# First 512 tokens through three transposing loads instead of matrix turns, in a fused linear-attention and dense-layer kernel

## The chip, the cores and the metric

The kernel runs on one core of a Trainium2 chip. The metric is the device time of one execution in microseconds, as the median of several runs. A core has five engines with instruction queues of their own: TensorE (PE, matmuls; PEld is its loading of weights), VectorE (DVE), ScalarE (ACT), GpSimd (POOL) and SyncE (SP). DMAs are issued here from SP's and ACT's queues; an engine that issues one is held for the time of the issue, and the data lands later.

## The reference

`x` is 2048 x 512 (tokens by features), in bf16, as all inputs are.

```python
g = sigmoid((x * gate_w).sum(-1, keepdims=True))
# A: linear attention, 32 heads of 16
q, k, v = heads(x @ wqkv)
phi(t) = concat(softmax(t @ w_phi), softmax(-(t @ w_phi)))   # per head, 16 + 16 features
kv = einsum("hsf,hsd->hfd", phi(k), v);  z = phi(k).sum(over s)
a = (phi(q) @ kv) / (phi(q) @ z + 1e-6)  @ wo
# B: a dense layer
b = relu(x @ w1) @ w2          # w1: 512 x 1376, w2: 1376 x 512
out = g * a + (1 - g) * b
```

## The kernel before

The 2048 tokens are 16 tiles of 128, or four chunks of 512. Every matmul over features needs `x` with the features on the partitions: that is the tile `XT` (128 partitions, 4 row pieces `j` of 128 features, 2048 tokens).

Each step is a named task on one engine, with its dependencies. The order of the tasks on each engine is written out in `ORDER`, one string an engine; a planner found it beforehand, and the numbers `dur`, `lat` and `boost` in the tasks are what it used. They are not read when the kernel is built: `schedule` only looks up the names, `number` gives each task a semaphore and a count (an engine's own semaphore, or one of its own for each DMA), and `emit` puts the waits ahead of the task. So an engine runs its tasks strictly in the order of its string, and a task that waits holds up all that stands behind it on the same engine; DMA issues stand in the strings of SP and ACT as well.

The tasks that matter here:

- `warm0` (line 258): matmuls of ones on PE, six of 512 columns, before any data is there.
- `x00` to `x03` (`load_x`, line 272): plain loads of the first four tiles of tokens into `XN`, a corner of `FT`, with the tokens on the partitions.
- `xt{m}{n}` (`pe_xt`, line 350): two matmuls each with the identity `IDN`, which turn two of the four 128 x 128 blocks of tile `m` into PSUM. `xe{m}{n}` (lines 362 on ACT, 365 on DVE) copy them into `XT`.
- `w1a0` to `w1a3`: the first 512 columns of `w1`, one load for each row piece `j`; `w1b` and `w1c` the other columns.
- `hh00` to `hh3` (`pe_h_first`, line 403): the four first units of `x @ w1` (512 of the 1376 columns), for tokens 0 to 255, row piece by row piece. `h0_0` to `h0_3` (`pe_h_rest`, line 409): the same units for tokens 256 to 511. `h{c}_{k}` (`pe_h`, line 397): the other units, chunk `c`, columns `k`. `rl*` (line 454, ACT) apply the relu and write `HT`.
- `f1_*`, `f0_*` (`pe_fold`, line 374): fold `w_phi`, made block-diagonal in `WBD`, into the key and query columns of `wqkv`, which `wkT` and `wqT` bring in transposed (`load_t`, line 277, an `dma_start_transpose`). `fe*` evict them into `WP`.
- `pr_*` (line 496): the folded projections of pairs of tiles, keys (`k0` to `k8`) and then queries (`q0` to `q8`); `ev` (523, ACT), `mx` and `mn` (527, 529, DVE), `t1` and `t2` (536, POOL), `ex` (541, ACT), `sm` and `rc` (DVE) and `nm` (550 and 573, POOL) make the two softmaxes of them. `v*` (476) and `kv*` (557) build `kv` and `z`.
- `tq*` (576) and `to*` (614): transposing DMAs from SBUF to SBUF, of 128 x 1024 and of 128 x 512 elements. `nd*` (600), `b*` (622), `a*` (628): attention output, second dense layer and `wo`, tile by tile. `oe*` and `st*` evict and store.

Chunks 1 to 3 of `x` come in by `load_t` as 512 tokens each (`x1`, `x2`, `x3`), straight into `XT`.

The turns of the first tokens and the copies behind them:

```python
XB, FB = ((0, 1), (6, 7), (0, 1), (6, 7)), (0, 1, 6, 7)

def pe_xt(q, m, n):
    for j in range(2 * n, 2 * n + 2):
        last = q.matmul(PS[:, XB[m][j // 2], (j % 2) * P:(j % 2 + 1) * P], XN[:, m, j * P:(j + 1) * P],
                        IDN[:, :], start=True, stop=True)
    return last
```

Of the kernel before, what the change touches and what calls it, by code (L numbers as in the profile page):

```python
# [6 lines left out]
ALU = mybir.AluOpType  # L7
# [42 lines left out]
    ),  # L50
# [98 lines left out]
def bass_gated_mix__linear_kernel_hedgehog__dense_activation_relu__prompt_kernel(  # L149
# [34 lines left out]
    WARM = (6 * (512,),)  # L184
# [3 lines left out]
    with ExitStack() as es:  # L188
# [32 lines left out]
        COLI = sb("COLI", [P, P], I32)  # L221
        IDN = sb("IDN", [P, P], BF16)
# [24 lines left out]
        add("iota_i", "pool", lambda q: q.iota(COLI[:, :], [[1, P]], channel_multiplier=0), dur=0.25, boost=800.0)  # L247
# [4 lines left out]
        XN = FT[:, NF - 2, :].rearrange("p (m d) -> p m d", d=D)  # L252
# [40 lines left out]
        load_x(0, "sp", 2.95)
        load_x(1, "act", 3.1)
        load_w(0, "sp", 3.2)
        load_w(1, "act", 3.4)
        load_w(2, "sp", 3.8)
        load_w(3, "act", 3.95)
        load_x(2, "sp", 4.0)
        load_x(3, "sp", 3.9)  # L300
        load("w1b", "sp", W1[:, :, 512:1024], w1r[:, :, 512:1024], dur=0.5, lat=5.0)
        load("wphi", "sp", WPS[:, :, :], A_w_phi.rearrange("(g hl) r c -> (hl r) g c", g=ND), dur=0.5, lat=4.9)
        load_t("wkT", WT[:, ND:2 * ND, :], A_wqkv[:, D:2 * D], (), 4.1, 2.7)
        load("w1c", "sp", W1[:, :, 1024:DFF], w1r[:, :, 1024:DFF], dur=0.5, lat=4.0)
        load("wv", "sp", WV[:, :, :], wvr, dur=0.5, lat=4.9)
        g.follow("iota_r", "iota_i")
        g.follow("iota_i", "iota_c")
        load_t("x1", XT[:, :, chunk(1)], x2[chunk(1), :], ("w1c",), 2.6, 2.3)
# [11 lines left out]
        add("ident", "dve", lambda q: q.tensor_tensor(IDN[:, :], ROWH[:, :], COLI[:, :], ALU.is_equal),  # L320
            ("iota_r", "iota_i"), dur=0.3, boost=2000.0)
# [12 lines left out]

        def pe_turn(q, b, blocks):
            for n, src in enumerate(blocks):
                last = q.matmul(PS[:, b, n * P:(n + 1) * P], src, IDN[:, :], start=True, stop=True)
            return last

# [6 lines left out]
        XB, FB = ((0, 1), (6, 7), (0, 1), (6, 7)), (0, 1, 6, 7)  # L346

        def pe_xt(q, m, n):
            for j in range(2 * n, 2 * n + 2):
                last = q.matmul(PS[:, XB[m][j // 2], (j % 2) * P:(j % 2 + 1) * P], XN[:, m, j * P:(j + 1) * P],  # L350
                                IDN[:, :], start=True, stop=True)
            return last

        for m in range(4):
            for n in range(2):
                add(f"xt{m}{n}", "pe", lambda q, m=m, n=n: pe_xt(q, m, n),
                    (f"x0{m}", "ident", f"xe{m - 2}{n}" if m > 1 else None), dur=0.2, boost=9000.0 - 10 * m)
            for n, eng in enumerate(("act", "dve")):
                xo = XT[:, 2 * n:2 * n + 2, m * P:(m + 1) * P]
                xi = PS[:, XB[m][n], 0:2 * P].rearrange("p (j t) -> p j t", j=2)  # L360
                if eng == "act":
                    add(f"xe{m}{n}", eng, lambda q, o=xo, i=xi: q.activation(o, i, ACT.Copy), (f"xt{m}{n}",), dur=0.35,
                        boost=9000.0 - 10 * m)
                else:
                    add(f"xe{m}{n}", eng, lambda q, o=xo, i=xi: q.tensor_copy(o, i), (f"xt{m}{n}",), dur=0.37,  # L365
                        boost=9000.0 - 10 * m)
        x0 = [f"xe{m}{n}" for m in range(4) for n in range(2)]
        xof = [x0, ["x1"], ["x2"], ["x3"]]


        HB = (3, 4, 5)
        def pe_fold(q, s, j, b):
            for i in range(ND):
                last = q.matmul(PS[:, b, i * P:(i + 1) * P], WT[:, s * ND + i, j * P:(j + 1) * P], WBD[:, i, :],  # L374
                                start=True, stop=True)
            return last

        for j in range(ND):
            b = FB[j]
# [361 lines left out]
```

## Time and profile before

| | |
|---|---|
| median of 3 runs | 151.77 us (151.59 to 152.13) |
| profiled execution: time, span | 151.63 us, 150.1 us |
| granted TensorE clock | 1.0 |
| PE busy | 145.3 us, 97% of the span |
| POOL, DVE, ACT busy | 109.4, 113.3, 92.2 us |
| PE's share of the chain that ended last | 94% |
| DMA | 15.59 MB, mean 104 GB/s |

The span is that of the instructions on the core; the execution's own time is longer by what lies around it. Lines such as L350 are lines of the kernel. "DMA ... to landing" counts from the start of an issue to the last of its 16 arrivals.

### The profile page before, as it was taken

What the parts mean: (1) busy time and instruction counts of PE and PEld (TensorE: products, weight loads), DVE (VectorE), ACT (ScalarE), POOL (GpSimd) and SP (SyncE); (2) the same over time, 40 slices, a digit from 0 to 9 for tenths busy, and PEclk for the clock granted to TensorE, in tenths of its full rate; (3) what the DMA queues carried; (4) which work ended last, traced back from release to release, by engine and by line L of the source; (5) the groups of instructions that cost most, each with busy time, mean ns of one, the idle gap of its engine ahead of it and who ended that gap; (6) DMA issues with size and microseconds to landing.
All of it is one profiled execution on the core that took longest, in us unless ns stands there. A gap on an engine that the chain in (4) does not pass through costs nothing.

```text
span 150.1 us, 2498 instructions
## 1 busy us (share of the span) xinstructions
PE 145.3 (97%) x936; PEld 74.3 (49%) x953; DVE 113.3 (76%) x168; ACT 92.2 (61%) x127; POOL 109.4 (73%) x71
## 2 busy tenths in 40 slices
PE   7999999999999999999999999999999999999992
PEld 2774444445554465445444545455444454454461
DVE  2423666999899949969999999999999969436301
ACT  3356769799969766599983937446564551310151
POOL 3000499999999999999999999998999791330000
PEclk9999999999999999999999999999999999999999
DMA  4999991000005603400000230975659884766251
GB/s 144 302 261 239 163 231 23 0 0 0 7 1 112 238 0 54 120 0 0 4 0 0 60 82 15 116 159 135 174 106 155 195 213 105 146 171 144 65 163 52
DMA packets 46307, 15.59 MB, mean 104 GB/s; under 512 B 39796, under 2 KB 46292, under 8 KB 46296
## 3 DMA queue, kind: packets, MB, share of 16 engines
q1 hardware_dynamic: 43560, 12.99, 42.1%
q10 hardware_dynamic: 2736, 2.45, 5.0%
q8 instruction: 7, 0.11, 0.3%
q14 instruction: 4, 0.03, 0.1%
HBM read 4.42 MB, written 2.11 MB: 43 GB/s over the span
## 4 chain that ended last, share of the span: by engine, by line
PE 94%; DMA 2%; issue 1%; DVE 1%
PE PS L622 24%; PE PS L397 23%; PE PS L496 18%; PE PS L476 9%; PE PS L628 9%; PE PS L557 3%; PE PS L600 3%; DMA FT<-in_A_x_dram 2%; PE PS L643 2%; PE PS L409 1%; PE PS L374 1%; PE PS L403 1%; PE PS L350 1%; PE PS L654 1%; DVE XT L365 1%
## 5 line engine op out<-in xcount | busy, mean ns | idle before, releaser
L536 POOL TENSOR_TENSOR TS<-PB,MX 128x1024 bf16<-128x1024 bf16 (+1 forms) x18 | 30.8, 1719 | 14.9 <-DVE MX L527 14.9
L397 PE MATMUL PS<-XT,W 128*128 128x512 bf16 (+1 forms) x156 | 38.3, 379 | 0.2
L622 PE MATMUL PS<-W,HT 128*128 128x512 bf16 (+1 forms) x160 | 37.5, 379 | 0.3
L543 DVE TENSOR_REDUCE ZB<-FT 128x128 f32<-128x2048 bf16 (+1 forms) x18 | 36.5, 2030 | 0.7 <-ACT FT L541 0.6
L541 ACT ACTIVATE FT<-TS 128x2048 bf16<-128x2048 bf16 (+1 forms) x18 | 30.9, 1718 | 7.7 <-POOL TS L536 7.5
L536 POOL TENSOR_TENSOR TS<-MN,PB 128x1024 bf16<-128x1024 bf16 (+1 forms) x18 | 30.9, 1723 | 0.8 <-DVE MN L529 0.8
L496 PE MATMUL PS<-WP,XT 128*128 128x512 bf16 x124 | 30.0, 379 | 0.2
L550 POOL TENSOR_TENSOR FT<-FT,SC 128x2048 bf16<-128x2048 bf16 (+1 forms) x9 | 29.5, 3286 | 0.0
L454 ACT ACTIVATE HT<-PS 128x512 bf16<-128x512 f32 (+1 forms) x44 | 24.7, 597 | 6.1 <-PE PS L397 4.9
L622 PEld LDWEIGHTS PS<-W,HT 128*128 128x128 bf16 (+1 forms) x165 | 15.5, 98 | 17.1
L527 DVE TENSOR_REDUCE MX<-PB 128x64 bf16<-128x1024 bf16 (+1 forms) x18 | 19.5, 1084 | 5.8 <-ACT PB L523 5.7
L397 PEld LDWEIGHTS PS<-XT,W 128*128 128x128 bf16 (+1 forms) x160 | 15.6, 101 | 16.5
L673 ACT ACTIVATE OSB<-PS,OMG 128x512 bf16<-128x512 f32 x15 | 10.2, 686 | 22.1 <-PE PS L628 22.1
L529 DVE TENSOR_REDUCE MN<-PB 128x64 bf16<-128x1024 bf16 (+1 forms) x18 | 19.3, 1083 | 2.6 <-ACT PB L523 2.6
L523 ACT ACTIVATE PB<-PS 128x1024 bf16<-128x1024 f32 (+1 forms) x18 | 16.7, 926 | 6.4 <-PE PS L496 3.4
L496 PEld LDWEIGHTS PS<-WP,XT 128*128 128x128 bf16 x128 | 12.1, 98 | 13.9 <-DVE WP L344 0.4
L573 POOL TENSOR_TENSOR FT<-FT,SR 128x1024 bf16<-128x1024 bf16 (+1 forms) x9 | 15.6, 1735 | 0.7
L476 PE MATMUL PS<-WV,XT 128*128 128x512 bf16 x62 | 16.0, 379 | 0.1
L628 PE MATMUL PS<-WO,OT 128*128 128x512 bf16 x58 | 14.2, 378 | 0.1
L609 DVE SCALAR_TENSOR_TENSOR OTM<-PS,EG,RD 128x256 bf16<-128x256 f32 x32 | 13.8, 462 | 0.2
L607 DVE RECIPROCAL RD<-PS 128x16 f32<-128x16 f32 x32 | 6.5, 234 | 9.0 <-PE PS L600 8.8
L485 ACT ACTIVATE VS<-PS 128x512 bf16<-128x512 f32 x16 | 9.6, 602 | 4.8 <-PE PS L476 4.7
(50 smaller groups left out, 97.5 us busy)
## 6 DMA issues: line engine op xcount, KB each, us to landing
out_dram<-OSB ACTq DMA_DIRECT2D x15, 128.0 KB, 2.2
W<-in_B_w_dram SPq DMA_DIRECT2D x1, 1280.0 KB, 6.9
W<-in_B_w_dram SPq DMA_DIRECT2D x1, 512.0 KB, 4.6
WV<-in_A_wqkv_dram SPq DMA_DIRECT2D x1, 512.0 KB, 4.6
WO<-in_A_wo_dram SPq DMA_DIRECT2D x1, 512.0 KB, 5.1
FT<-in_A_x_dram SPq DMA_DIRECT2D x3, 128.0 KB, 3.2
W<-in_B_w_dram SPq DMA_DIRECT2D x1, 352.0 KB, 3.8
W<-in_B_w_dram ACTq DMA_DIRECT2D x2, 128.0 KB, 3.3
```

Of the source, the lines that this page charges most:

```text
L397: last = q.matmul(PS[0:m, b, :], W1[:, j, k * P:k * P + m], XT[:, j, chunk(c)], start=(j == 0), stop=(j == ND - 1))
L454: add(f"rl{a}_{k}", "act", lambda q, a=a, k=k, b=b, rows=rows: q.activation(HT[0:rows, k, chunk(a)], PS[0:rows, b, :], ACT.Relu), (prev,), ...
L476: last = q.matmul(PS[:, 2, :], XT[:, j, m * P:(m + 1) * P], WV[:, j, :], start=(j == 0), stop=(j == ND - 1))
L496: last = q.matmul(PS[:, n, :], XT[:, j, m * P:(m + 1) * P], WP[:, s, j, :], start=(j == 0), stop=(j == ND - 1))
L527: add(f"mx_{J}", "dve", lambda q, sl=sl, w=w, i=pbg: q.tensor_reduce(MX[:, sl, 0:w * H], i, AX.X, ALU.max), (f"ev_{J}", old("t1")), dur=0. ...
L529: add(f"mn_{J}", "dve", lambda q, sl=sl, w=w, i=pbg: q.tensor_reduce(MN[:, sl, 0:w * H], i, AX.X, ALU.min), (f"ev_{J}", old("t2")), dur=0. ...
L536: add(f"{tn}_{J}", "pool", lambda q, o3=o3, a3=a3, b3=b3: q.tensor_tensor(o3, a3, b3, ALU.subtract), (f"{'mx' if sg == 0 else 'mn'}_{J}", ...
L541: add(f"ex_{J}", "act", lambda q, fs=fs, ts=ts, w=w: q.activation(FT[:, fs, 0:w * F], TS[:, ts, 0:w * F], ACT.Exp), (f"t1_{J}", f"t2_{J}", ...
L543: add(f"sm_{J}", "dve", lambda q, fs=fs, sl=sl, w=w: q.tensor_reduce(ZB[:, sl, 0:2 * w * H], FT[:, fs, 0:w * F].rearrange("p (g d) -> p g ...
L550: add(f"nm_{J}", "pool", lambda q, f3=f3, sl=sl, w=w: q.tensor_tensor(f3, f3, SC[:, sl, 0:2 * w * H].unsqueeze(2).to_broadcast([P, 2 * w * ...
L622: last = q.matmul(PS[:, ab, :], HT[0:r, k, m * P:(m + 1) * P], W2[0:r, k, :], start=(k == 0), stop=False)
L628: last = q.matmul(PS[:, ab, :], OT[:, m % NOT, t, :], WO[:, t, :], start=False, stop=(t == ND - 1))
```

## The change

Tiles 0 to 3 of the tokens no longer come in by four plain loads and sixteen matmuls. Three transposing loads write `XT` directly: `x00` (tile 0), `x01` (tile 1) and `x023` (tiles 2 and 3). With them go `XN`, the identity (`iota_i`, `ident`, `IDN`), `pe_xt` and the eight evictions. The transposing loads stand on SP's queue, with `w1a1` and `w1a3` between them; `w1a0` and `w1a2` are issued from ACT, and so are now `wphi`, which waits for `x01`, and `w1c`, which waits for `w1b`. The first units are split into eight tasks `hh{m}{j}`, by tile `m` and row piece `j`, in the order 00 02 01 10 12 11 03 13. There are seven warming matmuls instead of six. All five orders are written anew: on PE, `h0_7` now stands ahead of `pr_k0`, and the first `v` units come earlier. SP waits for four more stores at the end, all of them older than the last.

```diff
-        "x00 w1a0 w1a2 x02 x03 w1b wphi wkT w1c wv x1 x2 wqT x3 gw ...            # sp
+        "x00 w1a1 x01 w1a3 x023 w1b wkT wv x1 x2 wqT x3 gw ...
-        "x01 w1a1 w1a3 xe00 xe10 xe20 xe30 rl0_0 rl0_1 rl0_3 rl0_2 fe1_1 fe1_3 ...   # act
+        "w1a0 w1a2 wphi rl0_0 rl0_1 w1c rl0_2 rl0_4 rl0_5 fe1_1 fe1_3 rl0_3 ev_k0 ...
-        "warm0 xt00 xt01 xt10 xt11 hh00 hh01 hh1 hh2 xt20 xt21 xt30 xt31 hh3 h0_0 h0_1 h0_2 h0_3 h0_4 h0_5 f1_0   # pe
-        "f1_1 f1_2 f1_3 h0_6 pr_k0 h0_7 h0_8 pr_k1 h0_9 h1_0 pr_k2 ...
+        "warm0 hh00 hh02 hh01 hh10 hh12 hh11 hh03 hh13 h0_0 h0_1 h0_2 h0_3 h0_4 h0_5 h0_6 f1_2 f1_1 f1_0 f1_3 "
+        "h0_7 pr_k0 v0 h0_8 pr_k1 h0_9 v1 pr_k2 v2 h1_0 h1_1 pr_k3 ...
...
-    WARM = (6 * (512,),)
+    WARM = (7 * (512,),)
...
-        def load_x(m, eng, lat):
-            load(f"x0{m}", eng, XN[:, m, :], x0r[:, m, :], dur=0.45, lat=lat)
+        def load_x(name, t0, t1, dur, lat):
+            load_t(name, XT[:, :, t0 * P:t1 * P], x2[t0 * P:t1 * P, :], (), dur, lat)
...
+        load_w(0, "act", 2.0)
+        load_w(2, "act", 2.0)
+        load_x("x00", 0, 1, 0.9, 2.1)
+        load_w(1, "sp", 2.05)
+        load_x("x01", 1, 2, 0.9, 1.75)
+        load_w(3, "sp", 1.7)
+        load_x("x023", 2, 4, 1.34, 1.5)
+        load("wphi", "act", WPS[:, :, :], A_w_phi.rearrange("(g hl) r c -> (hl r) g c", g=ND), ("x01",), dur=0.5, lat=2.45)
...
+        load("w1c", "act", W1[:, :, 1024:DFF], w1r[:, :, 1024:DFF], ("w1b",), dur=0.5, lat=3.2)
...
-        x0 = [f"xe{m}{n}" for m in range(4) for n in range(2)]
-        xof = [x0, ["x1"], ["x2"], ["x3"]]
+        xof = [["x00", "x01", "x023"], ["x1"], ["x2"], ["x3"]]
...
-        add("hh00", "pe", lambda q: pe_h_first(q, 0, 0, P), ("xe00", "w1a0"), dur=0.22, boost=8500.0)
-        add("hh01", "pe", lambda q: pe_h_first(q, 0, P, 2 * P), ("xe10", "hh00"), dur=0.22, boost=8500.0)
-        prev = "hh01"
-        for j in range(1, ND):
-            add(f"hh{j}", "pe", lambda q, j=j: pe_h_first(q, j, 0, 2 * P), (f"xe0{j // 2}", f"xe1{j // 2}", f"w1a{j}", prev), dur=0.44,
-                boost=8500.0)
-            prev = f"hh{j}"
+        steps = [(m, j) for js in ((0, 2, 1), (3,)) for m in range(2) for j in js]
+        prev = None
+        for m, j in steps:
+            add(f"hh{m}{j}", "pe", lambda q, m=m, j=j: pe_h_first(q, j, m * P, (m + 1) * P), (f"x0{m}", f"w1a{j}", prev),
+                dur=0.22, boost=8500.0)
+            prev = f"hh{m}{j}"
...
-            for m in range(NT - NOS - 2, NT - 1):
+            for m in range(NT - NOS - 6, NT - 1):
                 q.wait_ge(sems[f"st{m}"], 16)
```

More of the change, by code (lines that the diff above doesn't have):

```diff
@@ L220, in bass_gated_mix__linear_kernel_hedgehog__dense_activation_relu__prompt_kernel @@
         COLH = sb("COLH", [P, P], I32)
-        COLI = sb("COLI", [P, P], I32)
-        IDN = sb("IDN", [P, P], BF16)
         ROWS = sb("ROWS", [P, P], I32)
@@ L246, in bass_gated_mix__linear_kernel_hedgehog__dense_activation_relu__prompt_kernel @@
         add("iota_r", "pool", lambda q: q.iota(ROWH[:, :], [[0, P]], channel_multiplier=1), dur=0.25, boost=900.0)
-        add("iota_i", "pool", lambda q: q.iota(COLI[:, :], [[1, P]], channel_multiplier=0), dur=0.25, boost=800.0)
         add("iota_c", "pool", lambda q: q.iota(COLH[:, :], [[1, 8], [0, DH]], channel_multiplier=0), dur=0.25,
@@ L251, in bass_gated_mix__linear_kernel_hedgehog__dense_activation_relu__prompt_kernel @@
             ap(VS, NT * NG * GZ, GV, [[GZ, NT * NG], [1, 1]]), 1.0), dur=0.7, boost=-1e4)
-        XN = FT[:, NF - 2, :].rearrange("p (m d) -> p m d", d=D)
         one = nc.const_aps.tensor(1.0, (P, 1), BF16).tensor
@@ L284, in bass_gated_mix__linear_kernel_hedgehog__dense_activation_relu__prompt_kernel @@
         w1r = B_w1.rearrange("(j p) n -> p j n", p=P)
-        x0r = x2[chunk(0), :].rearrange("(m p) d -> p m d", p=P)
         wvr = A_wqkv[:, 2 * D:3 * D].rearrange("(j p) n -> p j n", p=P)
-        def load_x(m, eng, lat):
-            load(f"x0{m}", eng, XN[:, m, :], x0r[:, m, :], dur=0.45, lat=lat)
+        def load_x(name, t0, t1, dur, lat):
+            load_t(name, XT[:, :, t0 * P:t1 * P], x2[t0 * P:t1 * P, :], (), dur, lat)
         def load_w(j, eng, lat):
             load(f"w1a{j}", eng, W1[:, j, 0:512], w1r[:, j, 0:512], dur=0.45, lat=lat)
[L293 to L308, printed above, removed]
+        load_w(0, "act", 2.0)
[6 more added lines that the diff above has]
+        load("wphi", "act", WPS[:, :, :], A_w_phi.rearrange("(g hl) r c -> (hl r) g c", g=ND), ("x01",), dur=0.5, lat=2.45)
+        load("w1b", "sp", W1[:, :, 512:1024], w1r[:, :, 512:1024], dur=0.45, lat=2.7)
+        load_t("wkT", WT[:, ND:2 * ND, :], A_wqkv[:, D:2 * D], (), 3.6, 2.0)
+        load("w1c", "act", W1[:, :, 1024:DFF], w1r[:, :, 1024:DFF], ("w1b",), dur=0.5, lat=3.2)
+        load("wv", "sp", WV[:, :, :], wvr, dur=0.5, lat=4.0)
+        g.follow("iota_r", "iota_c")
+        load_t("x1", XT[:, :, chunk(1)], x2[chunk(1), :], ("w1c",), 2.0, 2.8)
         load_t("x2", XT[:, :, chunk(2)], x2[chunk(2), :], (), 2.0, 4.3)
@@ L319, in bass_gated_mix__linear_kernel_hedgehog__dense_activation_relu__prompt_kernel @@
             ("iota_r",), dur=0.25)
-        add("ident", "dve", lambda q: q.tensor_tensor(IDN[:, :], ROWH[:, :], COLI[:, :], ALU.is_equal),
-            ("iota_r", "iota_i"), dur=0.3, boost=2000.0)
         add("blk", "dve", lambda q: q.tensor_tensor(GB[:, :], ROWS[:, :], COLH[:, :], ALU.is_equal),
@@ L332, in bass_gated_mix__linear_kernel_hedgehog__dense_activation_relu__prompt_kernel @@
         wbd = [f"wbd{j}" for j in range(ND)]
[L335 to L338, printed above, removed]
         def evict(name, eng, out_, b, deps, **how):
@@ L344, in evict @@
                 add(name, eng, lambda q: q.tensor_copy(out_, PS[:, b, :]), deps, dur=0.69, **how)
[L346 to L366, printed above, removed]
-        x0 = [f"xe{m}{n}" for m in range(4) for n in range(2)]
-        xof = [x0, ["x1"], ["x2"], ["x3"]]
+        FB = (0, 1, 6, 7)
+        xof = [["x00", "x01", "x023"], ["x1"], ["x2"], ["x3"]]
         HB = (3, 4, 5)
@@ L379, in bass_gated_mix__linear_kernel_hedgehog__dense_activation_relu__prompt_kernel @@
             b = FB[j]
-            war = [f"xe{2 + j // 2}{j % 2}"]
-            add(f"f1_{j}", "pe", lambda q, j=j, b=b: pe_fold(q, 1, j, b), ("wkT", *wbd, *war), dur=0.24,
+            add(f"f1_{j}", "pe", lambda q, j=j, b=b: pe_fold(q, 1, j, b), ("wkT", *wbd), dur=0.24,
                 boost=1800.0)
@@ L414, in bass_gated_mix__linear_kernel_hedgehog__dense_activation_relu__prompt_kernel @@
         GB4 = (*HB, 2)
-        add("hh00", "pe", lambda q: pe_h_first(q, 0, 0, P), ("xe00", "w1a0"), dur=0.22, boost=8500.0)
-        add("hh01", "pe", lambda q: pe_h_first(q, 0, P, 2 * P), ("xe10", "hh00"), dur=0.22, boost=8500.0)
-        prev = "hh01"
-        for j in range(1, ND):
-            add(f"hh{j}", "pe", lambda q, j=j: pe_h_first(q, j, 0, 2 * P), (f"xe0{j // 2}", f"xe1{j // 2}", f"w1a{j}", prev), dur=0.44,
-                boost=8500.0)
-            prev = f"hh{j}"
-        for line in (("warm0", "xt00", "xt01", "xt10", "xt11", "hh00", "hh01", "hh1", "hh2", "xt20", "xt21", "xt30", "xt31",
-                      "hh3"), ("xe00", "xe10", "xe20", "xe30"),
-                     ("ident", "shift", "xe01", "xe11", "xe21", "xe31", "blk", "row4", "mk")):
+        steps = [(m, j) for js in ((0, 2, 1), (3,)) for m in range(2) for j in js]
[4 more added lines that the diff above has]
+            prev = f"hh{m}{j}"
+        g.follow("warm0", "hh00")
+        for line in (("iota_r", "iota_c"), ("shift", "blk", "row4", "mk")):
             for a, b in zip(line, line[1:]):
@@ L538, in bass_gated_mix__linear_kernel_hedgehog__dense_activation_relu__prompt_kernel @@
             war = [(f"kv{m}" if jobs[jn - NF][0] == "k" else f"tq{m}") for m in jobs[jn - NF][1]] if jn >= NF else []
-            if jn == NF - 2:
-                war += [f"xt{m}{n}" for m in range(4) for n in range(2)]
             add(f"ex_{J}", "act", lambda q, fs=fs, ts=ts, w=w: q.activation(
```

67 rows, old and new, of the table ORDER are left out of this document.

## The prediction

> **What bounds the kernel now.** I read the page's first part, then the chain that ended last in its first 13 us, then SP's timeline and the tiles of the transposing loads, and last the table of windows.
>
> The page's first part (engine, busy us, share of the span, instructions):
>
> ```profile
> PE 145.3 (97%) x936; PEld 74.3 (49%) x953; DVE 113.3 (76%) x168; ACT 92.2 (61%) x127; POOL 109.4 (73%) x71
> ```
>
> PE is busy for 145.3 of 150.1 us, so time can only be saved where PE does work that isn't needed, or waits. The windows (us, then each engine's busy time) show that from 9.27 on there is next to none:
>
> ```profile
> 3.57:7.31 3.74, 3.54 (x36) 2.79 (x37) 1.70 (x6) 1.50 (x4) 0.00 (x0) 1.00 1.07 309
> 9.27:20.00 10.73, 10.68 (x61) 5.22 (x62) 4.54 (x5) 7.00 (x12) 3.06 (x2) 1.00 1.08 214
> ```
>
> Over 9.27 to 147.30 PE is busy for 137.12 of 138.03 us by the six windows that cover it: 0.9 idle. After it come 2.80 us in which the last tile is evicted and stored; the change doesn't touch them. So the change is decided by when PE has done its first units. The chain of waits (start, us, what):
>
> ```profile
> 0.74 2.78 DMA FT<-in_A_x_dram
> 3.52 0.05 issue
> 3.57 0.97 PE PS L350 x8
> 4.53 0.30 PE PS L403 x4
> 4.83 0.03 issue
> 4.86 1.27 PE PS L403 x12
> 6.13 0.24 PE PS L350 x4
> 6.37 0.02 issue
> 6.40 0.78 DVE XT L365 x2
> 7.18 0.14 issue
> 7.31 1.91 PE PS L409 x16
> 9.27 1.67 PE PS L397 x7
> ```
>
> A plain load of 128 tokens lands at 3.52; PE turns them (L350), ACT and DVE evict the turned blocks into `XT` (L362, L365), and only then can `hh*` (L403) run. The second half of the tokens goes the same way, and `h0_0` to `h0_3` (L409, tokens 256 to 511) start at 7.31. Call that start T. From T on everything is solid PE work, so the end moves as T does, one for one, unless something new is late behind it.
>
> **The change, part by part.**
>
> *PE's work.* Sixteen turns go. In their place nothing: the 32 pieces of 128 columns of `hh00` to `hh13` do the work of today's 20 (8 of 128, 12 of 256). L374 runs sixteen 128-column matmuls in 0.89 us, 0.056 each, so 32 take 1.79; today's take 8 x 0.056 + 12 x 0.109 = 1.76. The seventh warming matmul costs 0.43 (they start 0.43 apart, the last at 2.86): PE is free at 3.7 instead of 3.3. That is hidden by the wait for x01, w1a3 and x023, which all land later (below); were they early, it would cost 0.1 to 0.4. The eight evictions leave ACT and DVE, which wait at that stage anyway: nothing.
>
> *SP's queue decides T.* It now issues x00, w1a1, x01, w1a3, x023, w1b, wkT in this order; the `x` pieces and wkT are transposing loads. What such an issue costs (ns, min/median/max):
>
> ```profile
> L277 SPq DMA_TRANSPOSE XT<-in_A_x_dram x3: 1792/2319/3222, 11.5 to 19.1; - x3
> L277 SPq DMA_TRANSPOSE WT<-in_A_wqkv_dram x2: 2484/3014/3543, 4.1 to 16.6; - x2
> L576 SPq DMA_TRANSPOSE PHQ<-FT x16: 1231/1312/2256, 84.3 to 134.1; - x16
> L614 SPq DMA_TRANSPOSE OT<-OTM x16: 1188/1210/2272, 92.4 to 141.6; - x16
> L272 SPq DMA_DIRECT2D FT<-in_A_x_dram x3: 414/432/432, 0.7 to 2.6; - x3
> ```
>
> and from issue to landing (page, part 6, median us):
>
> ```profile
> FT<-in_A_x_dram SPq DMA_DIRECT2D x3, 128.0 KB, 3.2
> PHQ<-FT SPq DMA_TRANSPOSE x16, 2.8
> OT<-OTM SPq DMA_TRANSPOSE x16, 2.4
> ```
>
> No row has 128 tokens transposed from DRAM. From below: a quarter of the quickest load of 512 tokens, 1.79 / 4 = 0.45, no more than a plain load's 0.43. From above: OT, the same 128 KB, but from SBUF, 1.21. I take 0.9, a little nearer to OT, since OT and PHQ show that half the size doesn't halve it; both ends stay in the range. For x023 (256 tokens): PHQ's 1.31 above, 0.9 below, 1.2 taken. From issue to landing: x00 and x01 2.4 (OT) to 3.2 (FT), 2.8 taken; x023 2.8 (PHQ) to 4.45 (the quickest load of 512 tokens), 2.9 taken since PHQ is equally large. A plain issue is 0.43, gaps 0.04.
>
> So x00 is issued at 0.74 and lands at 3.55; w1a1 1.68, lands 4.7 (3.0 for such loads now); x01 2.15, lands 4.95; w1a3 3.09, lands 6.0; x023 3.56, lands 6.46. On ACT's queue w1a0 and w1a2 go out at 0.74 and 1.17 and land by 4.0. PE: `hh00` 3.7, `hh01` from 4.7, the three pieces of tile 1 from 4.95 to 5.65, `hh03` and `hh13` from 6.0 to 6.45, L409 at 6.5 to 6.6. T = 6.6 against 7.31: 0.7 gained. With an issue of 0.45, x023 goes out at 2.66 and T is 5.6; with 1.21, at 4.18 and T is 7.1, or 7.4 if it also takes 0.3 more to land.
>
> A queue of 256-byte pieces is also slower on the wire: with only a transposing load moving, 7.5 to 9.0, the trace has 275 GB/s; with plain loads, 11.0 to 12.0, 376 (last column):
>
> ```profile
> 7.50:9.00 1.50, 1.50 (x16) 1.34 (x15) 0.97 (x5) 1.05 (x2) 0.00 (x0) 1.00 1.24 275
> 11.00:12.00 1.00, 1.00 (x18) 0.87 (x15) 0.79 (x2) 0.57 (x2) 0.00 (x0) 1.00 1.08 376
> ```
>
> For x023's 256 KB that is 0.95 instead of 0.70 us, and it is in PHQ's 2.8 already. [...]
>
> *What is late next.* w1b goes out at 4.8 instead of 3.10. Now it lands at 7.70 with 1 MB ahead of it; by FT's fastest 2.8 plus 0.38 MB more at 376 GB/s it lands by 8.6, and at best at 7.9. `h0_4` wants it at 6.6 + 1.73 = 8.3: a wait of 0 to 0.3, 0.1 taken. wkT goes out at 5.3 and lands in 4.9 to 5.6: 10.2 to 10.9; the folds (L374) want it at 11.0. wphi now waits on ACT for x01 (5.0) and lands by 9.3 with its present 4.3; four WBD products of 0.28 end at 10.4, in time by 0.6. Behind it on ACT are the table load (1.28) and `rl0_0`: ready at 5.5 + 1.28 = 6.8, and `h0_0` ends at 7.1, so it is hidden. w1c waits on ACT for w1b, between `rl0_1` and `rl0_2`; `rl0_2` is wanted by `h0_6` at 10.2, and w1c, at 8.6 + 3.8 = 12.4, by `h0_8` at 15.5: hidden, by 1.5 and 3. wv lands at 13.3, wanted by `v0` at 14.6. x1 waits for w1c as now, lands by 12.4 + 5.9 = 18.3, wanted by `pr_k2` at 19.8.
>
> *The new order.* PE has the same units from there on. `h0_7` now stands before `pr_k0`, so `pr_k0` ends at 14.5, as now (14.54), and POOL, which is busy for 20.00 of 20 us in 20 to 40 and in 40 to 60, starts as now at 16.9. Its last k product (L550) ends at 86.2 and `kv15` (L557) starts at 87.4: 1.2 of cover, 0.5 when PE is 0.7 ahead. So POOL is next late, but not yet. I cost the rest of the new order at nothing: at best it wins back the 0.9 idle, at worst a unit waits for one eviction (L523, 1.0).
>
> Sum: 7.31 - 6.6 - 0.1 = 0.6. The profiled execution took 151.63 us, 1.53 more than its span; it becomes 149.5 + 1.53 = 151.03, and as the median stands 0.14 over the profiled one, 151.2 as a median. A difference of 0.3%, 0.45 us, is about what a measurement can tell from none.
>
> **The rivals.**
>
> *The issue is short.* Near 0.45, T is 5.6; then w1b, with the same bytes ahead of it as now, at 7.7 holds `h0_4` for 0.4, and POOL's cover is used up at 1.2 or so. About 1.1 gained: 150.7. For: the rows from DRAM are the ones of the same source. Against: OT. 10%.
>
> *The issue is as long as OT's.* T 7.1 to 7.4, w1b 0.2 late: 0 to 0.2 gained or lost, 151.8. For: OT has the same size. 20%. Here I also put a late clock: L258's first matmuls and L350's (up to 314 ns, 219 later) show PE slow until about 4.2; PE will wait between pieces just then. [...]
>
> *A transposing load is held by the copy ahead of it.* This is the slower side. wkT's issue, right behind w1b and wphi, took 3.54 us; wqT's, of the same size with no copy ahead, 2.48:
>
> ```profile
> 4.13 3.54 SPq L277 DMA_TRANSPOSE WT<-in_A_wqkv_dram  x1
> ```
>
> It ended at 7.67, when w1b landed (3.10 + 4.6). In the new queue x01 stands behind w1a1 and x023 behind w1a3. If each pays the 1.06, x023 goes out at 4.6 and its own issue is longer by 1.06 too: it lands at 8.6, 1.3 after 7.31: 153.0. It decides once the excess is over 0.4 a load. The same if the first such load of a run is dear. Against: wkT is 512 KB behind 512 KB, the copies here are 128 KB, and x1 was issued in 1.79 while wv still moved. 22%.
>
> That the change doesn't do what it says is excluded: the built program loads `XT` by three transposing loads, and no matmul of L350 is left.
>
> **How the numbers follow.** Forecast 48% (gains of 0.45 to 1.0: 150.8 to 151.3); short issue 10%; OT's issue or a late clock 20%; held loads 22%. Faster by over 0.3%: 48 + 10, less 4 for a forecast that falls short by a little: 54%. Same: 20 + 4 = 24%. Slower: 22%. The range begins at 150.5, the short issue's 1.7 - 0.4 without POOL's share, which leaves out next to nothing, and reaches to 152.3 (0.5 lost), which takes in OT's issue with a late w1b and the held loads that pay about half the excess: above it stay some 15%.
>
> **What would show it.** Right: SP's issues of 128 tokens at 0.9, x023 landing near 6.5, L409 from 6.6, no row of DVE or L350 in the chain's start, the last matmul near 146.6. Wrong: such an issue at 1.2 or more, L409 after 7.3, `h0_4` waiting for w1b by over 0.5, or a wait of L557 for POOL near 86.

## The result, and the profile after

| | before | after |
|---|---|---|
| median of 6 runs each, in turns on one chip | 152.26 us (151.59 to 152.84) | 153.57 us (153.34 to 153.72) |
| ratio | | 1.0086, 95% interval 1.0058 to 1.0114 |
| profiled execution: time, span | 151.63 us, 150.1 us | 153.6 us, 151.8 us |

The change makes the kernel slower by 1.3 us; 0.6 less was forecast. The profiled execution of before was one of its quicker ones, so the two profiles are 1.97 us apart.

The page's first part, of after: PE is busy for 1.0 us more, though sixteen turns are gone (its first units run slowly, below).

```profile
PE 146.3 (96%) x932; PEld 75.4 (50%) x950; DVE 110.7 (73%) x163; ACT 89.9 (59%) x123; POOL 108.9 (72%) x70
```

The chain of waits of after (start, us, what):

```profile
0.74 1.30 SPq L273
...
2.09 0.56 SPq L268
...
2.72 1.20 SPq L273
...
3.96 0.57 SPq L268
...
4.58 1.24 SPq L273
5.82 0.05 issue
5.86 5.14 DMA W<-in_B_w_dram
11.01 0.27 issue
11.28 2.54 PE PS L362 x11
```

L273 is a transposing load's issue, L268 a plain one's. The chain begins with SP alone: five issues, one after the other, and then `w1b`, which goes out at 5.86, lands at 11.01 and lets `h0_4` (L362) start at 11.28. In before the same chain ran over PE, DVE and `XT`, and `h0_4` started at 9.27. From 11.28 on PE is solid again; the windows of after show it in the row that answers to 9.27 to 20 of before, and over the seven rows from there to the end of the last matmul at 149.21 PE is busy for 137.0 of 137.9 us.

```profile
11.28:20.00 8.72, 8.67 (x51) 4.35 (x52) 2.78 (x4) 5.86 (x10) 0.18 (x1) 1.00 0.87 182
```

So the end moved with `h0_4`: it starts 2.0 us later, the last matmul ends 1.9 us later (149.21 instead of 147.30), and the span is 1.7 longer in these two executions. What PE does ahead of it, in after's timeline of PE:

```profile
4.75 3.59 PE L368 MATMUL PS<-XT,W 128*128 128x128 bf16 x32 [0.83 <-DMA XT<-in_A_x_dram]
8.14 2.77 PE L374 MATMUL PS<-XT,W 128*128 128x256 bf16 x16
11.28 2.54 PE L362 MATMUL PS<-XT,W 128*128 128x512 bf16 x11 [0.37 <-DMA W<-in_B_w_dram]
```

`hh*` (L368) runs at half speed (32 matmuls in 3.59 us, 0.11 each, where before has 0.056), and L374 is still slow until about 9.9, although the profile's granted clock reads 1.00 there. Yet L374 is over at 10.91, before `w1b` is there at 11.01: 0.37 of waiting is left. The two bounds are only 0.1 apart. Last, what the wire, that is the DMA engines together, carried (the last column, GB/s), of before and then of after:

```profile
2.00:4.00 2.00, 1.92 (x9) 0.73 (x8) 0.16 (x1) 1.28 (x2) 0.08 (x1) 1.00 0.91 297
4.00:6.00 2.00, 1.97 (x23) 1.61 (x22) 0.78 (x2) 0.76 (x2) 0.00 (x0) 1.00 1.04 303
6.00:8.00 2.00, 1.83 (x21) 1.36 (x19) 1.05 (x4) 0.78 (x3) 0.00 (x0) 1.00 1.18 282
```

```profile
2.00:4.00 2.00, 1.92 (x5) 0.44 (x3) 0.12 (x1) 0.00 (x0) 0.00 (x0) 1.00 0.94 226
4.00:6.00 2.00, 1.25 (x12) 1.25 (x13) 0.00 (x0) 0.16 (x1) 0.00 (x0) 1.00 0.65 155
6.00:8.00 2.00, 2.00 (x21) 2.00 (x20) 0.00 (x0) 1.12 (x1) 0.00 (x0) 1.00 1.05 163
```

From 4 to 8 us the DMA engines carry about half of what they carried in before (155 and 163 GB/s), while SP has something to issue all the time. The two stretches differ: from 4 to 6 the engines' busy share (the column before the last) falls to 0.65, so there they lack work; from 6 to 8 it reads 1.05, so there they are busy and move little. The DMA view of after's first 14 us (KB each, median us from issue to landing):

```profile
W<-in_B_w_dram SPq DMA_DIRECT2D x1, 512.0 KB, 5.1
...
W<-in_B_w_dram SPq DMA_DIRECT2D x2, 128.0 KB, 2.7
XT<-in_A_x_dram SPq DMA_TRANSPOSE x3, 3.5
```

### The profile page after: what moved, and what is told of

Read it like the earlier page. It is cut to its first block, busy times and chain, and to the rows that moved or that the text cites. A ratio compares the mean times of both kernels' runs of the same rounds, so it can differ in the third digit from the quotient of the medians.

```text
span 151.8 us, 2484 instructions
## 1 busy us (share of the span) xinstructions
PE 146.3 (96%) x932; PEld 75.4 (50%) x950; DVE 110.7 (73%) x163; ACT 89.9 (59%) x123; POOL 108.9 (72%) x70
## 3 DMA queue, kind: packets, MB, share of 16 engines
HBM read 3.89 MB, written 2.11 MB: 40 GB/s over the span
## 4 chain that ended last, share of the span: by engine, by line
PE 90%; DMA 3%; SPq 3%; issue 1%; DVE 0%
PE PS L584 23%; PE PS L362 22%; PE PS L460 18%; PE PS L440 9%; PE PS L590 8%; DMA W<-in_B_w_dram 3%; PE PS L519 3%; PE PS L562 3%; SPq L273 2%; PE PS L605 2%; PE PS L340 1%; SPq L268 1%; PE PS L616 1%; DVE OSB L626 0%
## 5 line engine op out<-in xcount | busy, mean ns | idle before, releaser
L362 PE MATMUL PS<-XT,W 128*128 128x512 bf16 (+1 forms) x152 | 37.0, 379 | 0.7 <-DMA W<-in_B_w_dram 0.4
L362 PEld LDWEIGHTS PS<-XT,W 128*128 128x128 bf16 (+1 forms) x160 | 15.6, 101 | 17.1 <-DMA W<-in_B_w_dram 0.4
```

The source lines that it names most:

```text
L362: last = q.matmul(PS[0:m, b, :], W1[:, j, k * P:k * P + m], XT[:, j, chunk(c)], start=(j == 0), stop=(j == ND - 1))
```

## The experiments

The theory, from the chain: SP feeds the wire nearly alone, a transposing issue holds it for 1.2 to 1.3 us, so `w1b` goes out 2.76 us later than before (5.86 instead of 3.10), and that is the loss. The rivals: PE's half speed; the new order of the units; copies and transposing loads that hold each other up; the transposing itself, on the wire. Ratios are to before, run in turns on the same chip, with 95% intervals; after's own is 1.0086.

**PE's half speed, and w1b on the other queue.** Three variants of the changed kernel. In e1 ACT issues `w1b`, behind `w1a2`, as soon as x00 has landed:

```diff
-        "x00 w1a1 x01 w1a3 x023 w1b wkT wv ...     # sp
+        "x00 w1a1 x01 w1a3 x023 wkT wv ...
-        "w1a0 w1a2 wphi ...                        # act
+        "w1a0 w1a2 w1b wphi ...
```

> w1b is issued from ACT's queue behind w1a2, released by x00, instead of from SP's behind x023. Theory (w1b's arrival at 11.01 is what held the first units): h0_4 no longer waits for it and follows the end of the slow L409-type matmuls (L374 of the changed kernel) at about 10.75 instead of 11.28, so 0.5 us less than the changed kernel. Rival (the half-speed matmuls and x023 alone set the time): w1b lands early and nothing else moves, under 0.2 us. Rival (copies behind a transposing load stall on any queue): w1b lands after 9.5 all the same.

In e2 matmuls of ones fill PE's waits, so that it stays at full speed:

```diff
-    WARM = (7 * (512,),)
+    WARM = (9 * (512,),)
-        "warm0 hh00 hh02 hh01 hh10 hh12 hh11 hh03 hh13 h0_0 ...
+        "warm0 hh00 hh02 hh01 hh10 hh12 hh11 fill0 hh03 hh13 fill1 h0_0 ...     # 2 + 2 matmuls of 512
```

> Nine warming matmuls instead of seven and two more of 512 columns before hh03 and before h0_0, which keep PE busy while it waits for loads. Theory (w1b bounds): the first units run at 0.056 and 0.109 us a matmul instead of 0.107 and 0.213, the second-half units (L374 of the changed kernel) end near 10, and h0_4 still starts at 11.3: no change of time, under 0.2 us. Rival (PE at half speed is the cause of the loss): 0.9 to 1.4 us less than the changed kernel.

e3 is both edits together.

> Both edits. Theory (three bounds in a row: w1b at 11.0, half-speed PE to 10.75, x023 at 8.07): h0_4 starts at 9.9 or so, 1.4 us less than the changed kernel and still 0.6 over the kernel before, which is x023's landing against its 7.31. Rival (something else of the new loads or order costs): less than 0.8 us is won.

Measured: e2 1.011 (1.0072 to 1.0149), the same as after within the intervals. PE's timeline of e2:

```profile
5.31 1.51 PE L376 MATMUL PS<-XT,W 128*128 128x128 bf16 x24 [0.80 <-DMA XT<-in_A_x_dram]
...
8.02 1.92 PE L382 MATMUL PS<-XT,W 128*128 128x256 bf16 x16
11.56 2.76 PE L370 MATMUL PS<-XT,W 128*128 128x512 bf16 x12 [1.62 <-DMA W<-in_B_w_dram]
```

PE is at full speed (24 matmuls in 1.51 us) and has finished L382 at 9.94, and then waits 1.62 us for `w1b`. The half speed is real, but it lies in the shadow of `w1b`: without it `h0_4` starts no earlier. This doesn't show that it would be harmless if `w1b` came in time; the 0.1 above says that it would then be the next bound. e1 is slower, not faster: 1.0304 (1.0244 to 1.0364). There `w1b` goes out at 4.22 and lands at 9.28, and `x023`, issued at 4.59 as in after, lands at 10.52 instead of 8.07:

```profile
10.56 3.60 PE L374 MATMUL PS<-XT,W 128*128 128x256 bf16 x16 [2.25 <-DMA XT<-in_A_x_dram]
```

PE waits 2.25 us for it and then runs L374 slowly. Here the granted clock shows it as well (the window's length, granted clock, DMA share, GB/s):

```profile
10.00:12.00 2.00, 0.50 1.31 258
```

So e1's loss is in part the late `x023` and in part the low clock behind the wait: `h0_4` starts 2.7 us later than in after, and the span is 3.7 longer. e3 ran at 1.0213 (1.0146 to 1.0281), between the two. Both expectations, 0.5 and 1.4 us less than after, failed: on ACT's queue `w1b` came early in e1, but at the cost of `x023`.

**The new order, and the order of the loads.** e4 keeps the new loads and takes the order of all that follows from before (that is its edit: the five strings from `h0_0` and `x1` on).

> The new loads and first units, and behind them all five orders of the kernel before. Theory (the loss is in the first 12 us, the new order behind it costs nothing): within 0.4 us of the changed kernel. Rival (part of the loss is the new order): 0.5 to 1.3 us less than the changed kernel.

Measured: 1.0111 (1.0073 to 1.0148). `w1b` goes out at 5.88 and lands at 11.21, `h0_4` starts at 11.26 after a wait of 0.96. L376 runs at full speed here (16 in 1.92 us), and still `h0_4` has to wait. The new order of the units neither costs nor gains anything that shows.

e5 puts the two copies ahead of the three transposing loads:

```diff
-        "x00 w1a1 x01 w1a3 x023 w1b wkT ...
+        "w1a1 w1a3 x00 x01 x023 w1b wkT ...
```

> SP issues w1a1 and w1a3 first, then x00, x01 and x023 back to back, then w1b; the rest is the changed kernel. Theory A (each change from a transposing load to a copy leaves the DMA engines nearly idle for 0.5 to 1 us, and the changed kernel has three of them ahead of w1b where this has one): w1b lands by 9.6 instead of 11.0, and 1.2 to 1.5 us are won. Theory B (only SP's issue times count: w1b is issued at 5.45 instead of 5.86): w1b lands at 10.6, 0.4 us won.

Measured: 1.0104 (1.0074 to 1.0134). SP's timeline of e5:

```profile
0.74 0.88 SPq L268 DMA_DIRECT2D W<-in_B_w_dram  x2
1.67 3.95 SPq L273 DMA_TRANSPOSE XT<-in_A_x_dram  x3
5.67 0.58 SPq L268 DMA_DIRECT2D W<-in_B_w_dram  x1
```

Three transposing issues without a copy between them take 3.95 with their gaps, 1.31, 1.25 and 1.30 each, as long as with copies between them (1.30, 1.20, 1.24). So it isn't the change from one kind to the other that costs: each such issue does. The plain ones ahead of them are shorter (0.41 and 0.42 instead of 0.56 and 0.57), so that `w1b` goes out 0.19 earlier, at 5.67. But it lands at 10.97, neither at 9.6 nor at 10.6 as the two theories had it, and nothing shows in the time.

**Is it the transposing, or SP's time?** In e6 plain loads of the same bytes stand in place of the three transposing ones; the turning is left out, so `XT` holds the tokens unturned. e7 is the same with each load cut in three, which holds SP about as long as the transposing issue did.

```diff
-            load_t(name, XT[:, :, t0 * P:t1 * P], x2[t0 * P:t1 * P, :], (), dur, lat)
+            load(name, "sp", XT[:, :, t0 * P:t1 * P], <the same rows, plain>, dur=dur, lat=lat)     # e6
+            for n, js in (("", slice(0, 2)), ("b", slice(2, 3)), ("c", slice(3, 4))):               # e7
+                load(name + n, "sp", XT[:, js, t0 * P:t1 * P], <the same rows, plain>, dur=dur, lat=lat)
```

> The three transposing loads become plain loads of the same bytes into the same places of XT, in 256- and 512-byte pieces; the turning of the tokens is left out. Both theories: x023 is issued at 2.7 and lands near 5.5, w1b is issued at 3.2 and lands near 7.7, PE starts h0_4 near 8.5 to 9, and the time is 2 to 2.7 us under the changed kernel and 0.3 to 0.8 under the kernel before. This is what the transposing loads cost in all.

> As the plain loads, but each in three pieces, so that SP is held for 1.3 to 1.6 us a piece of tokens as it is by the transposing loads, with no turning on the way (left out). Theory B (SP's issue time is the cause): w1b goes out near 6 as in the changed kernel and the time is within 0.5 us of the changed kernel's. Theory A (the wire stalls between transposing loads and copies): w1b lands 3.2 after its issue, near 9.3, h0_4 starts near 9.4, and 1.6 to 2 us of the loss are gone.

Measured: e7 1.007 (1.0044 to 1.0095), so plain loads are about as slow as the transposing ones when SP is held as long: `w1b` goes out at 6.10 and lands at 10.63. It isn't `w1b` that decides here, though. The chain of waits of e7 runs through the last piece of `x01`, issued at 3.69, and then through PE:

```profile
3.69 2.39 DMA XT<-in_A_x_dram
...
6.22 2.29 PE PS L370 x20
8.51 2.56 PE PS L376 x16
11.07 2.59 PE PS L364 x12
```

PE runs L370 at half speed (20 matmuls in 2.29) and is done with L376 after `w1b` has landed. So e7 shows that SP's time costs without any turning on the way; which of its late loads costs, it doesn't show. The windows of e7 carry as little as after's (155 and 163):

```profile
4.00:6.00 2.00, 1.43 (x12) 1.20 (x12) 0.00 (x0) 0.38 (x1) 0.00 (x0) 1.00 0.68 159
6.00:8.00 2.00, 1.79 (x19) 1.81 (x19) 0.40 (x3) 0.90 (x1) 0.00 (x0) 1.00 0.90 164
```

e6 1.0036 (1.0015 to 1.0057): with `w1b` out at 3.98, `h0_4` starts at 9.10, 2.2 us earlier than in after. Only about 0.8 us of it reaches the end, where 2 to 2.7 was expected and a time below that of before, since the next transfer is late: `wphi`, issued on ACT at 5.42, lands at 11.35, and the folds (L341) wait for its products in `WBD`. PE's timeline of e6:

```profile
9.10 2.76 PE L363 MATMUL PS<-XT,W 128*128 128x512 bf16 x12 [0.30 <-DMA W<-in_B_w_dram]
12.63 1.05 PE L341 MATMUL PS<-WBD,WT 128*128 128x128 bf16 x16 [0.76 <-DVE WBD L323]
```

**w1b's delay alone.** e9 is the kernel before, plain loads, turns and old order, with five loads of 4 KB as the only addition. They and `wphi` stand ahead of `w1b` on SP:

```diff
-        "x00 w1a0 w1a2 x02 x03 w1b wphi wkT ...
+        "x00 w1a0 w1a2 x02 x03 wphi d0 d1 d2 d3 d4 w1b wkT ...
+        for n in range(5):
+            load(f"d{n}", "sp", DUM[:, n, :], x0r[:, n % 4, 0:16], dur=0.45, lat=2.5)
```

> The kernel before, whole and without any transposing load of the first tokens; only wphi and five loads of 4 KB stand on SP's queue ahead of w1b, so that it is issued at about 5.9 instead of 3.10, as in the changed kernel. Theory (the time is lost because SP issues w1b late): w1b lands 4.6 to 5.1 after its issue, at 10.5 to 11.0; h0_4 starts then instead of at 9.27; 1.2 to 1.7 us slower than before, about as slow as the changed kernel. Rival (what costs is the transposing itself, the slow clock or the new order of the units): w1b has nothing ahead of it on the wire from 6.3 on, lands by 8.9, and the time is within 0.3 us of before.

Measured: 1.0074 (1.0051 to 1.0097), 0.95 us between the medians and 1.2 between the spans of the profiled executions. Its chain of waits:

```profile
6.00 4.18 DMA W<-in_B_w_dram
10.18 0.35 issue
10.53 1.67 PE PS L400 x7
```

`w1b` alone keeps `h0_4` from starting before 10.18, 0.9 later than in before. So the late issue of `w1b` is enough for most of what the change loses; the loads behind it on SP are late as well, but PE waits for none of them. In this execution PE was slow, too:

```profile
4.38 2.56 PE L406 MATMUL PS<-XT,W 128*128 128x128 bf16 x16
...
8.11 1.91 PE L412 MATMUL PS<-XT,W 128*128 128x256 bf16 x16 [0.28 <-DVE XT L368]
10.53 1.67 PE L400 MATMUL PS<-XT,W 128*128 128x512 bf16 x7 [0.52 <-DMA W<-in_B_w_dram]
```

L406 takes 2.56 where the same units take 1.70 in before, L412 starts 0.8 later, and only 0.52 of waiting for `w1b` is left. As in after, the two bounds lie close together, and `w1b` is the later one. The loss falls a little short of the expected 1.2 to 1.7; `w1b` needs 4.18 from issue to landing here, not 4.6 to 5.1. But it needs those 4.18 with next to nothing ahead of it, for between 6 and 8 the wire carries next to nothing:

```profile
6.00:8.00 2.00, 1.83 (x18) 1.29 (x15) 0.80 (x3) 0.66 (x2) 0.00 (x0) 1.00 0.44 45
```

In windows of half a us it carries 10 to 82 GB/s from 6.0 to 8.0, and 326 from 8.0 to 8.5. So about 2 of the 4.18 us pass before its bytes move in number.

**Why 5.14 and not 4.18?** In e11 `wkT`'s issue waits for `x023`, so that its pieces don't share the wire with `w1b`:

```diff
-        load_t("wkT", WT[:, ND:2 * ND, :], A_wqkv[:, D:2 * D], (), 3.6, 2.0)
+        load_t("wkT", WT[:, ND:2 * ND, :], A_wqkv[:, D:2 * D], ("x023",), 3.6, 2.0)
```

> The changed kernel, but wkT's issue on SP waits for x023 (8.07) instead of going out at 6.50. It tells how much of w1b's 5.14 from issue to landing is due to wkT's pieces beside it. If they are: w1b lands at 9.9 to 10.3, h0_4 starts at 10.8 or so (right behind L374 if the clock is low, else at 10.3), wkT lands at 12.5 to 13.0, as now, and the kernel is 0.4 to 0.8 us faster than the changed one. If the 5.14 is what such a load takes with nothing ahead of it: w1b lands at 11.0 still, wkT by 13.0, and the time is within 0.3 us of the changed kernel.

Measured: 1.0123 (1.0099 to 1.0146), `w1b` lands at 11.27, 5.40 after its issue. The idea was wrong: `wkT` beside it isn't what makes it slow. What remains is that `x023` is still landing until 8.07 to 8.09 in both kernels, while in e9 the last tokens, `x03`, have landed at 6.50. That fits, and so does e7 with 4.5 behind plain loads; but e6, with plain loads too, has 5.1, and e8 (below) 5.8, though all its tokens have landed at 5.00. So the last us of `w1b`'s landing time stays open. That `w1b` is the bound is borne out by e4, e5 and e11 as by e2: PE was ready earlier than in after and waited for it, 0.96, 1.42 and 1.13 us, and `h0_4` started at 11.26, 11.02 and 11.55.

In e13 `w1b` is cut into two loads of 256 columns, and `h0_4` and `h0_5` wait for the first alone (with e2's fillers, so it is held against e2):

```diff
-        load("w1b", "sp", W1[:, :, 512:1024], w1r[:, :, 512:1024], dur=0.45, lat=2.7)
+        load("w1b", "sp", W1[:, :, 512:768], w1r[:, :, 512:768], dur=0.45, lat=2.7)
+        load("w1bb", "sp", W1[:, :, 768:1024], w1r[:, :, 768:1024], dur=0.45, lat=2.7)
```

> The changed kernel with PE kept busy as in e2 (nine warming matmuls, four filling ones), and w1b as two loads of 256 columns, one behind the other on SP; h0_4 and h0_5 wait for the first half alone. It is to be held against e2 (1.011, h0_4 at 11.56 after 1.62 of waiting). Theory (the wait for w1b is what the change lost): the first half lands at 9.6 to 10.1, h0_4 starts at 10.0 to 10.2 and is 1.4 us earlier than in e2; wkT, issued 0.6 later, lands at 13.3 or so and is the next late: f1 was at 13.8 to 14.1 there and starts at 13.4 here, so that 0.3 to 0.7 of the 1.4 is kept: ratio 1.006 to 1.009. Rival (the wait for w1b only stands in for another one behind it, the folds' or POOL's): h0_4 is earlier but the time is that of e2, 1.011.

Measured: 1.0058 (1.004 to 1.0076), where e2 has 1.011. The first half lands at 9.76, 3.89 after its issue, and `h0_4` (L371) no longer waits. PE's timeline of e13:

```profile
8.49 1.92 PE L383 MATMUL PS<-XT,W 128*128 128x256 bf16 x16 [0.23 <-DMA XT<-in_A_x_dram]
10.46 2.54 PE L371 MATMUL PS<-XT,W 128*128 128x512 bf16 x11
12.84 1.06 PE L349 MATMUL PS<-WBD,WT 128*128 128x128 bf16 x16
```

It starts 1.1 us earlier than in e2, and some 0.8 us of that arrives at the end (the two intervals just touch); `wkT` landed at 12.42 and wasn't late. What is left against before is that L383 starts at 8.49 instead of 7.31, held by `x023`.

**Other places for the same loads.** In e10 ACT issues `w1b` at once behind `w1a2`, with no wait (e1's edit without the dependency on `x00`).

> The changed kernel with w1b issued by ACT right behind w1a2, with no wait: at about 1.65 instead of 5.86. Theory (the wire is half empty from 2 to 8 because one queue feeds it): w1b fills the gaps and lands by 7.5; x023 lands at 8.3 to 9.0; L374 starts then and h0_4 runs straight behind it, 10.2 to 10.9; 0.4 to 1.1 us faster than the changed kernel, still no faster than before. Rival (copies and a transposing load that are on the wire together hold each other up, as when ACT issued w1b at 4.22): x023 lands at 10 or later, h0_4 at 12 or later, slower than the changed kernel by over 0.7 us.

Measured: 1.0148 (1.0114 to 1.0181). Both landings come as the theory has them, `w1b` at 6.62 and `x023` at 8.80, but the time is the rival's. What the theory missed is that `w1a1`, issued by SP at 2.07, now lands at 7.03 instead of 4.97. PE waits for it, and goes on at half speed (24 matmuls in 2.88 us):

```profile
7.07 2.88 PE L368 MATMUL PS<-XT,W 128*128 128x128 bf16 x24 [1.82 <-DMA W<-in_B_w_dram]
9.74 2.07 PE L374 MATMUL PS<-XT,W 128*128 128x256 bf16 x16
```

e8 makes one transposing load of all 512 tokens, with the four row pieces and `w1b` behind it on SP, and ten warming matmuls:

```diff
-        "x00 w1a1 x01 w1a3 x023 w1b wkT ...
+        "x0 w1a0 w1a1 w1a2 w1a3 w1b wkT ...
```

> One transposing load of all 512 tokens first on SP, then w1a0 to w1a3 and w1b behind it on the same queue; row pieces in the order in which they come, ten warming matmuls. One issue of about 1.8 us instead of three of 1.25, one change from transposing to copying instead of three. Theory A: the tokens land by 4.5, the pieces between 6 and 7, w1b near 8.3; h0_4 at 9.3 or so: as the kernel before, within 0.4 us, 1.3 to 2 us under the changed kernel. Theory B: the same, from issue times alone, but no stall of the copies behind the load.

Measured: 1.0065 (1.004 to 1.009). The one issue takes 1.40 us for 512 tokens, hardly more than the 1.20 for 128, and all of them have landed at 5.00. But the row pieces come behind it, `w1a3` at 8.24, `w1b` goes out at 4.35 and lands at 10.16 instead of the expected 8.3, and `h0_4` starts at 10.49 instead of 9.3. Then PE waits once more, 0.67 for the folds: `wphi`, issued on ACT, is late, as in e6. The chain of waits of e8 has it:

```profile
5.02 7.61 DMA WPS<-in_A_w_phi_dram
```

e12 and e14 try to beat before: its turns stay for tokens 0 to 255, and one transposing load brings 256 to 511. In e12 that load stands second on SP, in e14 third, and ACT issues three of the row pieces:

```diff
-        "x00 w1a0 w1a2 x02 x03 w1b wphi wkT ...     # sp, before
+        "x00 x023 w1a3 w1b wphi wkT ...             # e12
+        "x00 w1a1 x023 w1b wphi wkT ...             # e14
-        "x01 w1a1 w1a3 xe00 xe10 xe20 xe30 ...      # act, before
+        "x01 w1a0 w1a1 w1a2 xe00 xe10 ...           # e12
+        "x01 w1a0 w1a2 w1a3 xe00 xe10 ...           # e14
```

> A version that may beat both. The kernel before with its turns for tokens 0 to 255, but tokens 256 to 511 by one transposing load that SP issues second (at 1.2), W1's row pieces 0 to 2 on ACT's queue, w1a3 and w1b on SP: w1b goes out at about 3.0, as before. Theory (feeding the wire early decides, and a transposing load is harmless where it holds up no issue that is wanted early): x023 lands by 6.3, eight turns and four evictions fall away from the path between the last landing and L409, which starts at 6.3 to 6.8 instead of 7.31, w1b lands at 7.7 to 8.3 and h0_4 starts at 8.3 to 8.8 instead of 9.27; 0.4 to 0.9 us faster than before. Rival (a transposing load beside copies slows both, so the wire takes longer for the same megabyte): x023 or w1a3 lands after 7.3, L409 starts later than 7.31 and the kernel is no faster than before, or slower by up to 1 us.

> As e12 (turns for tokens 0 to 255, one transposing load for 256 to 511), but in the order in which PE wants the pieces: SP issues x00, w1a1, x023, w1b, ACT x01, w1a0, w1a2, w1a3. w1b goes out at 3.0. Theory (a transposing load is harmless where it delays no wanted issue): w1a1 lands by 4.4, w1a2 by 5.3, w1a3 by 6.0, x023 by 6.5; L402 runs through without a wait, L408 starts at 6.4 to 6.7 instead of 7.31, w1b lands at 7.8 to 8.4 and h0_4 starts at 8.4 to 8.7 instead of 9.27: 0.5 to 0.8 us faster than before, ratio 0.995 to 0.997. Rival (copies and a transposing load slow each other on the wire): one of w1a2, w1a3 and x023 lands after 6.9, L408 starts after 7.0, ratio 0.998 to 1.004.

Measured: e12 1.0028 (0.9994 to 1.0062), e14 1.0033 (1.0007 to 1.0058): neither is faster than before. The rival has the times right; what it says of the loads came only in e14. In e12 `x023` lands at 5.97, early enough, but `w1a1`, now ACT's third issue, takes 4.06 us beside it (the third took 3.50 in before) and lands at 5.74 instead of 4.31; PE waits for it for 0.57, and L408 starts at 7.39, no sooner than in before. In the profiled execution of e14 it is worse: `x023` needs 7.11 us and `w1a3` 6.39, and L408 starts at 9.04. (That execution took 153.44 us; e14's begin at 151.77, so not all of them can have gone like this.) The chain of waits of e14, and the wire of e14 in the windows:

```profile
2.16 6.39 DMA W<-in_B_w_dram
```

```profile
4.00:6.00 2.00, 1.45 (x16) 0.91 (x14) 1.13 (x4) 0.62 (x2) 0.00 (x0) 1.00 1.06 131
6.00:8.00 2.00, 0.60 (x4) 0.32 (x4) 0.00 (x0) 0.00 (x0) 0.00 (x0) 1.00 1.16 178
```

The DMA engines are busy (the column before the last, 1.06 and 1.16) and move about half of what they moved in before. After looks like this from 6 to 8 (1.05, 163 GB/s), but not from 4 to 6, where the engines lacked work (0.65).

## Why the prediction was wrong

The mechanism by which the change was to gain exists: no turn and no eviction stands between a landing and `hh*`, the new order costs nothing that shows (e4), and POOL didn't become the bound (PE of after waits for it nowhere). The step that failed is the path through SP's queue. It was to bring T at 6.6 and `w1b` by 8.6, about when `h0_4` wants it (8.3); T came at 8.14 and `w1b` at 11.01, and `w1b` set the start of `h0_4`. The terms that it had wrong stand in "SP's queue decides T" and "What is late next":

- **The issue: 0.9 taken for 128 tokens, 1.20 and 1.30 measured**; 1.2 for `x023` was right (1.24). "A plain issue is 0.43" became 0.56 to 0.59 behind a transposing one. Together `w1b` went out at 5.86 instead of 4.8: 1.06 late, 0.74 of it in the transposing issues, 0.27 in the plain ones, the rest in gaps. The prediction called OT's 1.21 the upper end; it was the value, and after's row for all six loads into `XT` shows none below 1.20:

```profile
L273 SPq DMA_TRANSPOSE XT<-in_A_x_dram x6: 1202/1757/2972, 0.7 to 22.8; - x6
```

- **w1b's landing: 3.1 to 3.8 after its issue taken, 5.14 measured.** This is the larger error. The prediction reasoned that less stands ahead of `w1b` on the wire than in before, so that it lands sooner than 4.60. But the 4.60 were not for the most part a queue of bytes: with a nearly empty wire ahead of it e9 has 4.18. FT's 2.8 was the price of 128 KB. With 1.06 from the issue and 1.34 to the upper end of the landing, `w1b` came at 11.01 instead of 8.6.
- **x023: 2.9 from issue to landing taken, 3.49 measured**; issued 1.02 later as well, it landed at 8.07 instead of 6.46, and L374 started at 8.14 instead of 6.6. So T, which was to come 0.7 earlier than in before, came 0.83 later: with `w1b` in time there would still be no gain, as e13 shows (1.0058).
- **x00: 2.8 from issue to landing taken, 4.0 measured**; `hh00` started at 4.75 instead of 3.7, after the wait of 0.83 behind which PE ran at half speed. It cost nothing in after, since `w1b` came later still.

Then the sum turns over. `w1b` had 9.27 - 7.70 = 1.57 of cover in before. It came 3.31 later (2.76 in the issue, 0.54 in the landing); with 0.27 of issue rows between, 3.31 - 1.57 + 0.27 = 2.0 is what `h0_4` lost. The prediction gave the wait of `h0_4` for `w1b` 0 to 0.3 and called over 0.5 a sign of its being wrong. After shows 0.37, but only because PE came late and slow as well; with PE at full speed the wait is 1.62 (e2). Two more of its signs came: issues of 1.2 or more, and the units of L409 (L374 in after) starting later than 7.3.

The rivals:

- *The issue is as long as OT's* was right in its cause and wrong in its price: it followed the longer issue to T, by 0.5 or so, and w1b by "0.2 late" only. The slow PE that it calls a late clock came too, with `hh*` of after at 0.11 each, but e2 shows that it cost nothing beside the late `w1b`. What decides when PE comes to its full speed, no run shows: after a wait of 0.83, `hh*` of after ran at 0.11 each, and after a longer one, 1.44, those of e5 ran at 0.061 each (32 in 1.96), both behind the same seven warming matmuls.
- *A transposing load is held by the copy ahead of it*: it gave 153.0, near the 153.57, but by luck, for it came there by another way: an excess behind each copy and a late `x023`. `x01` and `x023` behind copies were issued in 1.20 and 1.24, and e5 without copies between them has 1.25 and 1.30: no excess. Only `wkT`'s issue right behind `w1b` was long again (4.31, 3.54 in before), and nothing waited for it.
- *The issue is short* is excluded by 1.20.

Putting `w1b` on the second queue made other loads late. With `w1b` on ACT, it landed 1.73 earlier in e1 and `x023` 2.45 later; in e10 it landed 4.39 earlier and `w1a1` 2.06 later. The issue times count beside the landings, too: 1.24 of issue for `x023` stands against 2.25 from its end to the landing, and the issue times sent `w1b` out 2.76 later.

## What to carry to other kernels

Where one queue feeds the wire at the start, add up its issue times first and the bytes second: a load that is put ahead of others costs them its issue, and here that hardly grew with the size (1.20 us for 128 tokens, 1.40 for 512). Take the landing time of a load from rows of its own size, and don't shorten it because less is ahead of it: here `w1b` took 4.60 in before, 5.14 in after, and still 4.18 in e9 with next to nothing ahead of it. When a step is removed from the path, ask at what time each later load is now issued, and how much of its cover that eats. When one late load is mended, look for the bound right behind it: here PE's half speed lay 0.1 us behind `w1b`.

## What the runs showed of the hardware

- At the head of SP's queue a transposing issue took 1.20 to 1.31 us for 128 tokens (after, e5), 1.24 to 1.33 for 256 (after, e12, e14) and 1.40 for 512 (e8, once): nearly a fixed price, about three plain issues of 0.43. So it feeds 128 KB in the time of 384 KB. Later loads of 512 tokens, behind others, held SP for 1.79 to 3.22 (before, after).
- A load of 512 KB took 4.18 us from issue to landing with a nearly empty wire ahead of it (e9), about 2 of them before its bytes moved in number. Each half of 256 KB took 3.9 to 4.1 (e13), 128 KB took 2.6 to 2.9 (after's row pieces on SP).
- Where ACT issued more copies while a transposing load moved, both landed later: `x023` took 3.49 in after, 4.76 in e12, 5.93 in e1 and 7.11 in e14, there with the DMA engines busy throughout; ACT's third copy took 4.06 in e12 and its fourth 6.39 in e14, where before's third took 3.50. Why, no run shows.
- The profile's granted clock read 1.00 while matmuls ran at half speed (after from 4.75 to about 9.9, 0.11 us for 128 columns instead of 0.056); in e1 it read 0.50 from 10 to 12.
